# Eight normalises of h moved to VectorE, the last output tile cut 384 + 128, and a new written-out order

## The chip, the cores and the metric

One NeuronCore of a Trainium2 chip runs the whole kernel. The metric is the device time of one execution in microseconds, lower is better; several executions are taken and their median counts. Five engines run side by side, each through its own queue in order: TensorE (PE), VectorE (DVE), ScalarE (ACT), GpSimd (POOL) and SyncE (SP), which here only issues DMAs.

## The reference

x is 2048 tokens by 512. All inputs and outputs are bf16.

```python
h  = x + A(layernorm(x))          # linear attention, 32 heads of 16, then wo
h2 = h + B(layernorm(h))          # gMLP, F = 1792, Fh = 896

def A(x, wqkv, wo):
    q, k, v = heads(x @ wqkv)
    pq, pk = phi(q), phi(k)       # where(t > 0, t + 1, exp(t)) + 1e-6
    o = (pq @ (pk.T @ v)) / (pq @ sum(pk) + 1e-6)
    return o @ wo

def B(x, w_in, w_sp, b_sp, w_out):
    z = gelu(x @ w_in)
    g = w_sp @ layernorm(z[:, Fh:]) + b_sp[:, None]
    return (z[:, :Fh] * g) @ w_out
```

## The kernel before

The 2048 tokens are 16 tiles of 128 rows (n = 0 to 15), in eight pairs p and four groups of four (gq, tg). The work runs in five stages that overlap.

**Attention, keys.** For each tile of x, DVE takes statistics (`stats` L568, `aggr` L572), ACT or POOL makes 1/sqrt(var + eps) (`rstd_pool` L587 and L589 for pairs), DVE normalises (`normalise`, L603). The first six tiles are transposed by PE (L633, copied out by ACT, L640), the other ten by a transposing DMA on SP (L625). Then PE makes keys (`kv_proj`, L715), the feature map phi runs on ACT and DVE (L692, L694, L695, L698, L701), and PE sums key times x (L747). **Attention, queries.** `q_proj` (L729) and the denominators (`den`: L829, ACT L834 and L836, spread L844, ACT L854, DVE L856 and L859). **h.** PE projects (L879), DVE adds to x in place (L884), then the second layernorm: statistics on DVE, rstd on POOL, and, with `N2_ACT = range(16)`, `minus` on POOL (L614, L615: -mean times rstd) and the normalise itself on ACT (`normalise_act`, L610). The result goes to one of four buffers `xn` and from there through a transposing DMA on SP to hT (L625). A buffer is free for another tile when its DMA has read it. **gMLP in.** PE makes z2 from each tile (L911, two pieces of 512 and 384 columns), ACT takes gelu (L916), DVE takes statistics (L920) and normalises 896 columns (L603 again); PE makes z1 from groups of four tiles (L942) and ACT takes gelu (L947). **Mixing and out.** PE multiplies by w_sp (L981, 448 matmuls), DVE adds the bias (L988) and multiplies (L990), PE projects (L999), DVE adds h (L1005) and SP stores (L1007). The last tile is projected in two halves of 256 columns. w_sp reaches the chip through 64 transposing DMAs on SP (L957), of which the first 16 lie ahead of those of h in SP's queue. On POOL's queue stand the loads of wv, win, wo, the bias and wout (L492), each behind the last transpose that it must wait for.

**What sets the order.** Every operation is recorded by `op` with its operands; `schedule` then takes two lists written out by hand. ORDER lists all operations by number: each engine runs its own in the order in which they stand there. SLOT says which buffer each temporary tile takes (PSUM banks `ps`, buffers `e`, `xn`). From these the program derives the semaphores: an engine waits at an operation for its operands and for the earlier users of its buffer, and everything later on that engine waits behind it. The costs that stand at each `op` matter only to assertions and bookkeeping, as the lists decide the order.

Of the kernel before, what the change touches and what calls it, by code (L numbers as in the profile page):

```python
# [5 lines left out]
FP32 = mybir.dt.float32  # L6
BF16 = mybir.dt.bfloat16
ACT = mybir.ActivationFunctionType
ALU = mybir.AluOpType

P = 128
# [1 line left out]


ORDER = [
# [36 lines left out]
]  # L52
SLOT = [
# [6 lines left out]
]  # L60


# [292 lines left out]
def bass_sequential_preLN__linear_attn_block__mixer_gmlp__prompt_kernel(  # L355
# [11 lines left out]
    _, S, D = A_x.shape  # L367
# [15 lines left out]
    A_STATS = ()  # L383
    R_POOL = (4, 6, 8, 10, 12, 14)
    COPY_DVE = ()
    LN1 = [[0], [1], [2], [3], [4, 5], [6, 7], [8, 9], [10, 11], [12, 13], [14, 15]]
    N2_ACT = range(16)
    VIA_ACT = ((0, 0), (1, 0), (2, 0), (3, 0))

    x_dram, out_dram = A_x[0], out[0]  # L390
# [210 lines left out]
    def normalise(dst, src, st_row, k, rs, n=512, negative=False):  # L601
        m = st_row[k:k + 1]
        op("dve", dve_c(n, 4) + 0.1, lambda e: e.tensor_scalar(dst.ap(), src.ap(), m.ap(), rs.ap(),  # L603
                                                               op0=ALU.add if negative else ALU.subtract,
                                                               op1=ALU.mult),
           r=[src, m, rs], w=[dst])


    def normalise_act(dst, src, rs, nm, n=512):
        op("act", act_c(n, 2) + 0.04, lambda e: e.activation(dst.ap(), src.ap(), ACT.Identity, bias=nm.ap(), scale=rs.ap()),  # L610
           r=[src, rs, nm], w=[dst])

    def minus(m, rs, nm):
        op("pool", 0.25, lambda e: e.tensor_scalar(nm.ap(), m.ap(), -1.0, None, op0=ALU.mult), r=[m], w=[nm])  # L614
        op("pool", 0.25, lambda e: e.tensor_tensor(nm.ap(), nm.ap(), rs.ap(), ALU.mult), r=[nm, rs], w=[nm])  # L615
# [31 lines left out]
    for grp in LN1:  # L647
        rs = small([len(grp)], FP32)
        for i, n in enumerate(grp):
            rs_of[n] = rs[i:i + 1]  # L650
        for n in grp:
            if n in A_STATS:
                stats_act(n)
                continue
            stats(x[n, :], Row(st_x, n))
            first[n] = g.ops[-1]
            aggr(Row(st_x, n), 6)
            if n in CENTRED:
                m, c = st_x[n, 6:7], xc[n, :]
                op("dve", dve_c(512, 4) + 0.1, lambda e, n=n, m=m, c=c: e.tensor_scalar(  # L660
                    c.ap(), x[n, :].ap(), m.ap(), None, op0=ALU.subtract), r=[x[n, :], m], w=[c])
                transposed(n, lambda c=c: c, xcT, True)
        if grp[0] in A_STATS:
            rstd_act(st_x[grp[0], 7:8], rs.all(), 1.0 / D)
        elif grp[0] in R_POOL:
            rstd_pool(st_x[grp[0]:grp[-1] + 1, 7], rs.all(), len(grp))
        else:
            rstd_act(st_x[grp[0]:grp[-1] + 1, 7], rs.all())
        rs_op[grp[0]] = g.ops[-1]
        for i, n in enumerate(grp):  # L670
            d = xn1[n, :]
            normalise(d, x[n, :], Row(st_x, n), 6, rs[i:i + 1], negative=n in A_STATS)
            transposed(n, lambda d=d: d, xT, n in X_BY_PE)

    for gate, n, cost, count in ((first[0], 512, 2 * MM, 3), (rs_op[0], 512, 2 * MM, 1), (tr_op[0], 256, MM, 2),
# [340 lines left out]
                for n in range((tg - 1) * TPG, tg * TPG):  # L1016
                    project(n, [(0, D)])
    for n in range((NG - 1) * TPG, NT):
        project(n, [(0, D)] if n < NT - 1 else [(0, D // 2), (D // 2, D)])


    g.schedule()
# [55 lines left out]
```

## Time and profile before

| | us |
|---|---|
| median of 3 runs (lowest, highest) | 244.26 (243.93, 244.29) |
| the profiled execution, its own time | 243.96 |
| its span, first to last instruction | 242.2 |
| granted TensorE clock | 1.00 of full speed |

The profile is one execution. 1.76 us of its time lie outside the span. Its views show the busy time of each engine (a matmul's end is modelled, so PE can look busy while it waits a little), the chain of waits that ended last, groups of instructions by line and shape, and the instructions in order of time. Line numbers are those of the kernel before; in the kernel after they are 2 to 13 higher.

### The profile page before, as it was taken

How to read it: one execution, taken by the hardware profiler on the slowest of the kernel's cores; microseconds unless marked ns; L12 is line 12 of the kernel's file. 1: busy time of each engine (PE TensorE's matmuls, PEld its weight loads, DVE VectorE, ACT ScalarE, POOL GpSimd, SP SyncE). 2: the span in 40 equal slices, each digit the busy share in tenths (PEclk: the TensorE clock that was granted, in tenths of full speed). 3: DMA queues.
4: the chain of work that ended last, by engine and by line, in shares of the span. 5: the costliest groups of instructions: out<-in, count | busy, mean ns of one | idle time of the engine just before them, and what ended most of it. 6: DMA issues, size and time to landing. Idle time of an engine off the chain costs nothing.

```text
span 242.2 us, 3026 instructions
## 1 busy us (share of the span) xinstructions
PE 238.3 (98%) x1175; PEld 108.8 (45%) x1175; DVE 135.2 (56%) x269; ACT 85.1 (35%) x107; POOL 34.1 (14%) x87
## 2 busy tenths in 40 slices
PE   8999999999999999999999999999999999999995
PEld 3544443433444444445444444444444444444443
DVE  4999654589999967656533223251332513322443
ACT  3875744898588598564500010000000000000000
POOL 5316021002316542122100000000000000000000
DMA  6920459954324231459344444446200100000022
GB/s 199 321 43 18 94 106 337 232 122 96 46 43 128 47 46 22 87 119 231 88 108 92 107 86 95 100 108 94 83 0 0 65 24 0 0 0 3 0 87 87
DMA packets 55598, 21.57 MB, mean 89 GB/s; under 512 B 49472, under 2 KB 54720, under 8 KB 55584
## 3 DMA queue, kind: packets, MB, share of 16 engines
q1 hardware_dynamic: 54640, 17.05, 32.7%
q0 software_dynamic: 944, 4.33, 5.5%
q8 instruction: 9, 0.15, 0.3%
q14 instruction: 5, 0.04, 0.1%
HBM read 7.47 MB, written 2.10 MB: 40 GB/s over the span
## 4 chain that ended last, share of the span: by engine, by line
PE 91%; DVE 4%; DMA 2%; ACT 2%; SPq 1%; issue 0%
PE ps L981 40%; PE ps L942 10%; PE ps L911 10%; PE ps L999 10%; PE ps L747 6%; PE ps L879 5%; PE ps L715 5%; PE ps L729 4%; DMA xh<-in_A_x_dram 2%; DVE small L568 1%; SPq L492 1%; DVE xT_pq_z L698 1%; DVE xh L884 0%; DVE xT_pq_z L859 0%; DVE e L695 0%; PE ps L844 0%
## 5 line engine op out<-in xcount | busy, mean ns | idle before, releaser
L981 PE MATMUL ps<-wsp,pk_xn_z 128*128 128x512 bf16 x336 | 73.8, 379 | 0.0
L988 DVE TENSOR_TENSOR e<-ps,e 128x512 bf16<-128x512 f32 x28 | 19.4, 691 | 66.0 <-PE ps L981 66.0
L981 PEld LDWEIGHTS ps<-wsp,pk_xn_z 128*128 128x128 bf16 x336 | 32.8, 98 | 39.5
L942 PE MATMUL ps<-hT,win 128*128 128x512 bf16 x112 | 26.6, 379 | 0.0
L911 PE MATMUL ps<-win,hT 128*128 128x512 bf16 (+1 forms) x128 | 26.0, 353 | 0.0
L999 PE MATMUL ps<-wout,xT_pq_z 128*128 128x512 bf16 (+1 forms) x119 | 24.7, 367 | 0.0
L981 PE MATMUL ps<-wqkv_wsp,pk_xn_z 128*128 128x512 bf16 x112 | 24.3, 379 | 0.0
L947 ACT ACTIVATE xT_pq_z<-ps 128x1024 bf16<-128x1024 f32 (+1 forms) x16 | 14.4, 913 | 23.9 <-PE ps L942 23.9
L568 DVE BATCH_NORM_STATS2 small<-xh 128x6 f32<-128x512 bf16 x32 | 20.7, 678 | 3.3 <-DMA xh<-in_A_x_dram 3.3
L920 DVE BATCH_NORM_STATS2 small<-pk_xn_z 128x6 f32<-128x512 bf16 (+1 forms) x32 | 18.3, 611 | 7.2 <-ACT pk_xn_z L916 7.1
L692 ACT ACTIVATE e<-ps 128x1024 bf16<-128x1024 f32 x16 | 16.5, 1029 | 9.7 <-PE ps L715 6.1
L911 PEld LDWEIGHTS ps<-win,hT 128*128 128x128 bf16 x128 | 12.5, 98 | 12.7 <-ACT e L854 0.3
L916 ACT ACTIVATE pk_xn_z<-ps 128x896 bf16<-128x896 f32 x16 | 14.5, 914 | 8.9 <-PE ps L911 8.8
L1005 DVE TENSOR_TENSOR e<-ps,xh 128x512 bf16<-128x512 f32 (+1 forms) x17 | 11.2, 660 | 11.3 <-PE ps L999 11.3
L999 PEld LDWEIGHTS ps<-wout,xT_pq_z 128*128 128x128 bf16 x119 | 11.6, 98 | 12.8
L981 PEld LDWEIGHTS ps<-wqkv_wsp,pk_xn_z 128*128 128x128 bf16 x112 | 11.0, 98 | 13.2
L942 PEld LDWEIGHTS ps<-hT,win 128*128 128x128 bf16 x112 | 10.9, 98 | 12.6 <-ACT pk_xn_z L916 0.4
L589 POOL TENSOR_TENSOR small<-small 128x2 f32<-128x2 f32 x22 | 16.0, 727 | 1.2
L587 POOL TENSOR_SCALAR small<-small 128x2 f32<-128x2 f32 x22 | 6.4, 297 | 67.6 <-DVE small L572 67.4
L747 PE MATMUL ps<-pk_xn_z 128*128 128x512 bf16 x64 | 15.6, 379 | 0.0
L729 PE MATMUL ps<-xT_pq_z,wqkv_wsp 128*128 128x512 bf16 x64 | 15.5, 380 | 0.0
L715 PE MATMUL ps<-wqkv_wsp,xT_pq_z 128*128 128x512 bf16 x64 | 15.3, 379 | 0.0
(72 smaller groups left out, 191.0 us busy)
## 6 DMA issues: line engine op xcount, KB each, us to landing
out_dram<-e SPq DMA_DIRECT2D x15, 128.0 KB, 1.7
win<-in_B_w_in_dram POOLq DMA_DIRECT2D x1, 1792.0 KB, 9.2
xh<-in_A_x_dram SPq DMA_DIRECT2D x5, 256.0 KB, 4.7
wqkv_wsp<-in_A_wqkv_dram SPq DMA_DIRECT2D x2, 512.0 KB, 5.7
wout<-in_B_w_out_dram POOLq DMA_DIRECT2D x1, 896.0 KB, 6.4
wsp<-in_B_w_sp_dram SPq DMA_TRANSPOSE x48, 2.9
xh<-in_A_x_dram SPq DMA_DIRECT2D x1, 512.0 KB, 6.2
wqkv_wsp<-in_A_wqkv_dram POOLq DMA_DIRECT2D x1, 512.0 KB, 4.8
```

Source lines behind the costliest of these rows:

```text
L568: op("dve", dve_c(512), lambda e: e.bn_stats(s6.ap(), src.ap()), r=[src], w=[s6])
L589: return op("pool", 0.7, lambda e: e.tensor_tensor(dst.ap(), dst.ap(), h.ap(), ALU.pow), r=[dst, h], w=[dst])
L692: op("act", act_c(n), lambda e: e.activation(lo.ap(), t(flat).ap(), ACT.Exp), r=[t()], w=[lo])
L715: i = e.matmul(t(bank(ti)).ap(), lhsT=lhs.ap()[:, c, :], rhs=rhs.ap()[:, c, :], start=(c == 0), stop=(c == KD - 1))
L729: r_ = e.matmul(t(bank(i)).ap(), lhsT=lhs.ap()[:, c, :], rhs=rhs.ap()[:, c, :], start=(c == 0), stop=(c == KD - 1))
L747: r = e.matmul(txk[h](bank(i)).ap(), lhsT=xx.ap()[:, c * P:(c + 1) * P], rhs=kk.ap(), start=(n == 0), stop=(n == NT - 1))
L911: k = e.matmul(t(bank(i)).ap()[:, 0:b - a], lhsT=l.ap()[:, c, :], rhs=win[c, a:b].ap(), start=(c == 0), stop=(c == KD - 1))
L920: op("dve", dve_c(b - a), lambda e, s6=s6, src=src: e.bn_stats(s6.ap(), src.ap()), r=[src], w=[s6])
L942: k = e.matmul(t(bank(i)).ap(), lhsT=l.ap()[:, c, :], rhs=r_.ap()[:, c, :], start=(c == 0), stop=(c == KD - 1))
L981: k = e.matmul(t(bank(0)).ap(), lhsT=l.ap()[:, s - a, :], rhs=r_.ap()[:, s - a, :], start=(s == 0), stop=(s == NT - 1))
L988: op("dve", dve_c(512), lambda e: e.tensor_tensor(gb().ap(), t(bank(0)).ap(), bsp().ap()[:, tg * GW:(tg + 1) * GW], ALU.add), r=[t(), bsp( ...
L999: k = e.matmul(t(bank(0)).ap()[:, 0:b - a], lhsT=l.ap()[:, fc, :], rhs=wout[fc, a:b].ap(), start=(fc == 0), stop=(fc == KF - 1))
```

## The change

Three things change. The statistics and rstd stay where they were, but for tiles 8 to 15 the normalise of h runs on DVE (`normalise`) in place of ACT (`normalise_act`), and `minus` on POOL falls away for those four pairs. The last output tile is computed, added and stored as 384 and 128 columns. ORDER and SLOT are new lists throughout (796 operations in place of 804), so operations of all stages stand in another order, on every engine. `normalise_pool` and the tuples `N1_POOL` and `N1_ACT` are new as well; the tuples are empty, so tiles of x go the same way as before.

```diff
 ORDER = [
...
 SLOT = [
...
     COPY_DVE = ()
+    N1_POOL = ()
+    N1_ACT = ()
     LN1 = [[0], [1], [2], [3], [4, 5], [6, 7], [8, 9], [10, 11], [12, 13], [14, 15]]
-    N2_ACT = range(16)
+    N2_ACT = range(8)
...
+    def normalise_pool(dst, src, m, rs):
+        op("pool", 0.9, lambda e: e.tensor_scalar(dst.ap(), src.ap(), m.ap(), rs.ap(), op0=ALU.subtract,
+                                                  op1=ALU.mult), r=[src, m, rs], w=[dst])
...
-            normalise(d, x[n, :], Row(st_x, n), 6, rs[i:i + 1], negative=n in A_STATS)
+            if n in N1_POOL:
+                normalise_pool(d, x[n, :], st_x[n, 6:7], rs[i:i + 1])
+            elif n in N1_ACT:
+                nm = small([1], FP32)
+                minus(st_x[n, 6:7], rs[i:i + 1], nm.all())
+                normalise_act(d, x[n, :], rs[i:i + 1], nm.all())
+            else:
+                normalise(d, x[n, :], Row(st_x, n), 6, rs[i:i + 1], negative=n in A_STATS)
...
-        project(n, [(0, D)] if n < NT - 1 else [(0, D // 2), (D // 2, D)])
+        project(n, [(0, D)] if n < NT - 1 else [(0, D - P), (D - P, D)])
```

What the new lists move, as far as the prediction speaks of it:

- The keys of tiles 6 to 15 stand earlier among the work of PE: those of tile 10 come before the first half of the second group's queries has its partner (one `q_proj` pair, L729, fewer ahead of them).
- On DVE, the normalise of x's tile 10 has three more normalises and two more steps of phi ahead of it.
- The load of wo stands ahead of wv and win on POOL.
- All projections of tiles 12 to 15 (L879) now stand ahead of the denominators of the third group (L829); the first z2 of tile 2 (L911) follows directly on the spread L844 and takes the PSUM banks that held the z2 of tile 0.
- For tiles 8 to 15 the normalises on DVE take turns in the `xn` buffers: tile 10 takes the buffer of 8, 14 that of 10, 11 that of 9, 13 that of 11, so DVE waits there until the transposing DMA of the earlier tile has read it. On SP the transposes still go in the order 0 to 15.
- The last z2 tiles (13, 14, 12, 9, 15) and with them the need for the last hT tiles come earlier on PE; the tail of the mixing's first column (L981, token tiles 8 to 15) comes later.

84 rows, old and new, of tables (ORDER, SLOT) are left out of this document.

## The prediction

> **What bounds the kernel now.** I read the page's busy times first, then the chain of waits, then the windows by stage.
>
> ```profile
> span 242.2 us, 3026 instructions
> PE 238.3 (98%) x1175; PEld 108.8 (45%) x1175; DVE 135.2 (56%) x269; ACT 85.1 (35%) x107; POOL 34.1 (14%) x87
> PE 91%; DVE 4%; DMA 2%; ACT 2%; SPq 1%; issue 0%
> ```
>
> PE is busy 98% of the span and carries 91% of the chain that ended last. No edit removes a matmul, so the time can change only where PE waits, or before its first or after its last matmul.
>
> ```profile
> 10.59:57.00 46.41, 46.26 (x257) 20.41 (x258) 34.65 (x69) 33.32 (x39) 8.39 (x13) 1.00 0.60 138
> 57.00:70.00 13.00, 13.00 (x69) 5.73 (x70) 12.95 (x21) 9.58 (x12) 3.46 (x8) 1.00 0.36 63
> 70.00:90.00 20.00, 20.00 (x98) 9.45 (x97) 18.01 (x44) 15.48 (x21) 10.90 (x29) 1.00 0.32 66
> 90.00:120.50 30.50, 30.50 (x153) 14.77 (x151) 19.83 (x45) 18.75 (x22) 6.72 (x13) 1.00 0.52 106
> 120.50:239.74 119.24, 119.22 (x560) 54.45 (x558) 42.05 (x72) 2.05 (x2) 0.00 (x0) 1.00 0.24 56
> ```
>
> Each row is a stretch of the span: its length, then the busy time of PE, its weight loads, DVE, ACT and POOL (instructions in brackets), the clock, and the DMAs' share and GB/s. From 10.59 to 239.74 PE misses 0.15 + 0.02 us. A busy PE is not quite a fed one, but little is left to win there. DVE is the engine next to full: 12.95 of 13.00 us in 57 to 70 and 18.01 of 20.00 in 70 to 90. Into this stage the change puts eight more DVE instructions. The clock is 1.00 everywhere.
>
> ```profile
> 30.30 0.86 PE ps L715 x4
> ...
> 56.99 0.40 PE ps L844 x4
> ...
> 65.27 0.33 PE ps L829 x4
> ...
> 66.57 3.03 PE ps L911 x16
> 69.59 0.33 PE ps L844 x4
> 69.92 1.83 PE ps L942 x8
> ...
> 239.76 0.42 DVE e L1005
> ```
>
> This is the chain in order of time. Four 512-column matmuls take 0.86 us, one z2 tile 3.03 / 2 = 1.51.
>
> **The engines' prices.** Groups by form; the third number after the count is the mean ns of one.
>
> ```profile
> L610 ACT ACTIVATE xn<-xh,small 128x512 bf16<-128x512 bf16 x16 | 12.5, 805 | 4.5 <-POOL small L615 4.2 <-DMA hT<-xn 0.3
> L603 DVE TENSOR_SCALAR pk_xn_z<-xh,small 128x512 bf16<-128x512 bf16 x16 | 6.2, 400 | 0.0
> L614 POOL TENSOR_SCALAR small<-small 128x2 f32<-128x2 f32 x8 | 2.1, 260 | 1.7 <-DVE small L572 1.2
> L615 POOL TENSOR_TENSOR small<-small 128x2 f32<-128x2 f32 x8 | 2.3, 297 | 0.5
> L695 DVE TENSOR_SCALAR e<-e 128x1024 bf16<-128x1024 bf16 x16 | 6.7, 419 | 7.4 <-ACT e L694 5.6 <-ACT e L692 1.8
> L698 DVE TENSOR_TENSOR xT_pq_z<-e 128x1024 bf16<-128x1024 bf16 x8 | 5.4, 684 | 0.1
> L859 DVE TENSOR_TENSOR xT_pq_z<-xT_pq_z,ps 128x1024 bf16<-128x1024 bf16 x4 | 4.8, 1204 | 0.0
> L568 DVE BATCH_NORM_STATS2 small<-xh 128x6 f32<-128x512 bf16 x32 | 20.7, 678 | 3.3 <-DMA xh<-in_A_x_dram 3.3
> L1005 DVE TENSOR_TENSOR e<-ps,xh 128x512 bf16<-128x512 f32 x15 | 10.4, 691 | 10.9 <-PE ps L999 10.9
> L1005 DVE TENSOR_TENSOR e<-ps,xh 128x256 bf16<-128x256 f32 x2 | 0.8, 424 | 0.4 <-PE ps L999 0.3
> ```
>
> The move takes 8 x 0.805 = 6.4 us from ACT and 4 x (0.260 + 0.297) = 2.2 us from POOL, and gives DVE 8 x 0.400 = 3.2 us. None of these sums is on the chain; they matter through PE's waits. An instruction on DVE frees the queue about 0.08 us before its recorded end, so one normalise occupies it for 0.32, and likewise one statistics (L568) for 0.6, one product of phi or of the denominators (L698) for 0.6, the wide one with PSUM (L859) for 1.1.
>
> **Step 1, start to 10.59.** The first loads, statistics, transposes and keys stand in the same order on PE; on DVE one statistics of a later tile precedes tile 3's normalise, which PE needs only when its keys of tile 2 are done. Cost 0; bounds 0 and, if the later tile's data is late, +0.3 (one statistics, less that cover).
>
> **Step 2, keys, 10.59 to 45.** The keys of tiles 6 to 15 wait for transposing DMAs, and PE now asks earlier.
>
> ```profile
> 23.17 0.40 DVE L603 TENSOR_SCALAR pk_xn_z<-xh,small 128x512 bf16<-128x512 bf16 x1
> ...
> 30.40 2.58 SPq L625 DMA_TRANSPOSE xT_pq_z<-pk_xn_z  x2
> xT_pq_z<-pk_xn_z SPq DMA_TRANSPOSE x10, 2.5
> ```
>
> Tile 10's keys start at 30.30 before; after, one q_proj pair (1.73) fewer stands ahead, so PE asks at 28.57. Its normalise started at 23.17 at the end of a full DVE queue; three more normalises (0.96), one more L695 (0.34) and one more L698 (0.60) stand ahead now: 25.07, and up to 0.3 more if DVE waits for a rstd of POOL. It ends by 25.5 to 25.8, and the DMA lands 2.5 later, at 28.0 to 28.3: 0.3 to 0.6 us of slack, where there were 4. The transposes after it follow each 1.29 (2.58 / 2) apart, tile 15's at 34.5 to 34.8, for keys that PE reaches after 35. I take 0; the bounds are 0 and +0.5. wv, wo and win start up to 0.8 us later behind tile 15, with wo first; nothing in PE's order needs them sooner than before.
>
> **Step 3, 57 to 72.** Here I expect a wait.
>
> ```profile
> 66.01 0.67 ACT L834 ACTIVATE wsp<-ps,small 128x512 f32<-128x512 f32 x1
> ...
> 68.65 1.90 ACT L916 ACTIVATE pk_xn_z<-ps 128x896 bf16<-128x896 f32 x2
> ```
>
> The denominators of the third group (L829, 65.27 in the chain) wait for one more projection tile (0.86): about 66.1. L834 then starts at about 66.5 in place of 66.01, and the steps behind it on ACT up to the first gelu (L916) follow 0.5 later: gelu starts at 69.15 and frees its banks at about 70.1. PE does the same work up to there, the moved projection included, and reaches the end of the spread at 69.92; in the new order the next instruction wants just those banks: 0.2 us. The first z2 piece of tile 3 then waits for the copy L854 two ACT instructions on, less than 0.1 more. I take +0.3. Upper bound +0.8 (the gelus late by half a us more). Lower bound -0.3: the chain shows PE held before 56.99 by about 0.3, by the same kind of wait (sum into x, then the spread); I find that wait in the new order as well and so count no gain.
>
> **Step 4, 72 to 120.5: the moved normalises.**
>
> ```profile
> 54.81 1.22 DVE L884 TENSOR_TENSOR xh<-ps,xh 128x1024 bf16<-128x1024 f32 x1
> ...
> 87.10 0.92 DVE L603 TENSOR_SCALAR pk_xn_z<-pk_xn_z,small 128x896 bf16<-128x896 bf16 x2
> hT<-xn SPq DMA_TRANSPOSE x16, 2.5
> 92.62 10.78 SPq L625 DMA_TRANSPOSE hT<-xn  x6
> ```
>
> From its first addition of h (54.81) to the fourth normalise of z2 (87.10 + 0.92) DVE has almost no idle time. The new queue, from the first addition (1.5 earlier) to the normalise of tile 8, holds the same additions and statistics, four normalises more (1.3), a phi step (0.6) and a step of the denominators (0.6 to 1.1) more, one statistics of z2 less (0.5): 88.0 - 1.5 + 2.2 = 88.7 at its end. From there a chain through the buffers begins: transpose of 8 (2.5), normalise of 10 (0.4), its transpose, and likewise 9, 11, 13; with 0.1 per handover tile 11 lands at about 96.0, 13's DMA is issued at 96.5, 14's and 15's at 1.3 us steps behind it, and 15 lands at about 101.7. Before, the last of six transposes was issued about 1.3 before 92.62 + 10.78 = 103.4. PE reaches the first instruction that needs tile 15 (z1 of the fourth group) after 9 z2 tiles and one piece (14.5), 15 z1 blocks and 4 projections (19 x 0.86 = 16.3) and four pieces of mixing (1.7): 70.2 + 32.5 = 102.7. Cover: 1.0 us. All eight normalises then cost 0, hidden beside PE's work; if the cover is gone, each us on DVE's chain is one on PE's. The wait for buffers stands in DVE's queue, so behind it wait the normalises of z2 for the mixing; PE asks for the first of these at about 82.6 and has it by 82.2, later ones are covered by more. I take 0; bounds 0 and +1.5 (the chain late by 2.5, one whole transpose).
>
> **Step 5, 120.5 to 239.74.** 119.22 of 119.24 us busy, same matmuls, banks still in turn: 0. wsp's transposes start earlier than at 103.44 if step 4 holds.
>
> **Step 6, the tail.**
>
> ```profile
> 239.76 0.42 DVE L1005 TENSOR_TENSOR e<-ps,xh 128x256 bf16<-128x256 f32 x1 [0.34 <-PE ps L999]
> ...
> 240.21 0.33 SPq L1007 DMA_DIRECT2D out_dram<-e  x1
> out_dram<-e SPq DMA_DIRECT2D x15, 128.0 KB, 1.7
> out_dram<-e SPq DMA_DIRECT2D x2, 64.0 KB, 1.5
> ```
>
> The 384 columns end 0.38 (7 x 0.054) before the last matmul, at 239.36 with PE's end unmoved. Their addition, 0.56 between 0.424 and 0.691, ends at 239.94; its store is issued at 239.97 and holds SP for 0.33. The 128 columns' addition (0.29 by the same line) cannot start before 239.85 and ends at 240.14, a hair before 240.18 as it was, but its store waits for SP until 240.30 in place of 240.21: +0.09. Landing stays at 1.5 by the nearest row; bounds 1.4 (the line from 128 to 64 KB continued) and 1.7. Step: +0.1, bounds 0 and +0.3.
>
> The Trainium skill (DMA: Bandwidth & Descriptors, Specifications) gives 512 B as the smallest transfer at line rate and says that below it the engine does a read-modify-write; 128 columns are 256 B a row, 256 were 512 B. By it the last store would be slower, and no run here shows such a store yet.
>
> **Sum.** 0 + 0 + 0.3 + 0 + 0 + 0.1 = +0.4 us on the profiled execution's 243.96 (span 242.2 and 1.76 around it): 244.36. The runs' median is 244.26, 0.30 above the profiled one, whose time lies near the lowest, 243.93; three runs don't say how much of this is chance. I add 0.24 of it: **244.6**, between 244.36 and 244.66.
>
> **The rivals.**
> - **DVE's buffer chain is late (slower).** One mechanism: DVE waits in order for transposes to free `xn`, and tile 15 reaches hT after PE asks for z1 of group four. It decides from 1.0 us of delay before tile 8's normalise. For it: DVE has 0.05 of 13 us free in 57 to 70, and POOL's small instructions vary while DVE is full (rows below). Against: my queue count goes by rows, and DVE has 10 us free after 90. At 2 us of delay PE loses 1.0 to 1.5: 245.6 to 246.1.
>
> ```profile
> 17.43 0.86 POOL L587 TENSOR_SCALAR small<-small 128x2 f32<-128x2 f32 x1 [5.24 <-DVE small L572]
> 81.12 0.22 POOL L587 TENSOR_SCALAR small<-small 128x2 f32<-128x2 f32 x1 [3.15 <-DVE small L572]
> ```
>
>   The same instruction takes 0.22 or 0.86: up to 0.64 of the 1.0 us cover. The Trainium skill (Advanced Engine Details and Errata, VectorE Performance Modes) says that a VectorE instruction in a two-port mode and GpSimd block each other; by it the moved normalises would make rstd on POOL slower, and the trace agrees that rstd varies.
> - **The keys wait for tile 10 (slower, small).** If DVE's queue before 25 is 0.8 later, PE waits 0.3 to 0.5 in step 2: 244.9 to 245.1, still the forecast's side of the bound below or just past it.
> - **PE's early waits go (faster).** The wait before 56.99 vanishes, the gelu wait of step 3 does not come and no other does: -0.3 - 0.4 from the forecast, 243.9; with the profile's offset gone too, 243.6. Little more is there to win: PE misses 0.17 us by the records and about 0.3 by the chain.
> - **The change does nothing that shows.** Its edits are real (eight instructions change engine), but all are covered: 244.3, inside the forecast's range.
>
> **Chances.** 0.2% is 0.49 us, about what a measurement here can tell from no change: faster is below 243.77, slower above 244.75. Forecast and the covered case, 244.0 to 245.0: 0.58, of which 0.48 within and 0.10 above. Buffer chain late: 0.24, all above. Tile 10's wait on top of step 3: 0.08, 0.06 above. Early waits gone: 0.10, 0.08 below. Together 0.08 faster, 0.52 same, 0.40 slower. The range leaves out the last part of the faster case and the far end of the buffer chain: 243.7 to 246.2.
>
> **What would show it.** Step 2: no wait of L715 for a transpose near 28 us. Step 3: PE idle or its weight loads waiting for ACT's L916 near 70, about 0.2 us. Step 4: L603 normalises of 512 columns at 88 to 97, tile 15's transpose landing before 102.5, PE unbroken to the end. Step 6: last store issued about 0.55 after PE's last matmul, landing in about 1.5. Wrong would be: PE waiting on hT's DMA or on L603 between 82 and 116, or PE's last matmul more than 0.8 us from 240.0.

## The result, and the profile after

The changed kernel takes 244.64 us (median of 22 runs, 244.47 to 246.06), the kernel before in the same job 244.29 (22 runs, 243.89 to 247.58). The ratio is 1.0021, 95% interval 1.0012 to 1.003: slower by 0.3 to 0.7 us. The forecast was 244.6. The profiled execution took 244.63, its span is 242.9; that of before had 243.96 and 242.2.

First the page of the kernel after: span, engines, and the chain by engine.

```profile
span 242.9 us, 3014 instructions
PE 238.8 (98%) x1175; PEld 108.7 (45%) x1175; DVE 136.8 (56%) x277; ACT 79.5 (33%) x99; POOL 31.6 (13%) x79
PE 85%; DVE 7%; DMA 3%; ACT 1%; POOL 1%; SPq 1%; issue 0%; DVEq 0%
```

DVE has eight instructions more and ACT eight fewer, as the diff says. ACT's sum falls by 5.6 us and POOL's by 2.5, DVE's rises by 1.6 (forecast 6.4, 2.2 and 3.2; the sums don't set the time). PE's share of the chain falls from 91% to 85%, since the chain now runs through DVE up to the keys of tile 10. The windows of after, by the stretches of the forecast (columns as there), show where:

```profile
10.59:57.00 46.41, 46.13 (x256) 20.49 (x257) 34.74 (x69) 32.04 (x38) 8.03 (x13) 1.00 0.59 136
57.00:70.00 13.00, 13.00 (x70) 5.43 (x68) 13.00 (x24) 10.29 (x14) 2.84 (x8) 1.00 0.34 72
70.00:90.00 20.00, 19.77 (x100) 9.28 (x97) 19.62 (x48) 12.69 (x17) 9.04 (x21) 1.00 0.22 55
90.00:120.50 30.50, 30.50 (x152) 14.70 (x150) 20.97 (x50) 16.97 (x19) 7.11 (x13) 1.00 0.61 122
```

PE misses 0.28 us in the first stretch (0.15 before) and 0.23 between 70 and 90 (nothing before); it runs unbroken from 90 to the tail. The chain of waits of after, in order of time, names both places:

```profile
2.68 4.57 DMA xh<-in_A_x_dram
...
26.28 2.41 DMA xT_pq_z<-pk_xn_z
28.69 0.14 issue
28.82 1.02 PE ps L728 x4
...
69.42 0.93 ACT pk_xn_z L929
70.39 1.04 PE ps L924 x4
```

These are tile 10's keys (L728 here, L715 before), which wait for their transposing DMA, and the second z2 (L924, L911 before), which waits for the first gelu.

**How big the two waits are.** The recorded end of a matmul is modelled, so idle time by the records understates a gap; the distance of starts doesn't. PE in time order, after:

```profile
26.75 1.89 PE L760 MATMUL ps<-pk_xn_z 128*128 128x512 bf16 x8
28.82 1.02 PE L728 MATMUL ps<-wqkv_wsp,xT_pq_z 128*128 128x512 bf16 x4 [0.19 <-DMA xT_pq_z<-pk_xn_z]
...
69.78 0.40 PE L857 MATMUL ps<-wsp,small 32*128 32x512 bf16 x4
70.39 1.04 PE L924 MATMUL ps<-win,hT 128*128 128x512 bf16 x4 [0.23 <-ACT pk_xn_z L929]
```

Eight matmuls at 0.216 take 1.73, so PE was ready at 28.48 and started at 28.82: **0.35** lost (0.19 by the records). The other wait stands behind the spread of the third group. There PE of before has:

```profile
69.53 0.40 PE L844 MATMUL ps<-wsp,small 32*128 32x512 bf16 x4
69.85 1.90 PE L942 MATMUL ps<-hT,win 128*128 128x512 bf16 x8
```

Before, the next matmul came 69.85 - 69.53 = 0.32 after the spread's start, here it comes 70.39 - 69.78 = 0.61 after it: **0.29** lost.

**A wait that went.** PE and ACT of before, then PE and ACT of after, at the spread of the fourth group (L844, L857):

```profile
55.85 1.03 PE L729 MATMUL ps<-xT_pq_z,wqkv_wsp 128*128 128x512 bf16 x4
56.99 0.40 PE L844 MATMUL ps<-wsp,small 32*128 32x512 bf16 x4
...
56.22 0.63 ACT L836 ACTIVATE wsp<-wsp 128x512 bf16<-128x512 f32 x1
```

```profile
57.99 1.03 PE L892 MATMUL ps<-pk_xn_z,xT_pq_z 128*128 128x512 bf16 x4
58.95 0.40 PE L857 MATMUL ps<-wsp,small 32*128 32x512 bf16 x4
...
57.71 0.63 ACT L849 ACTIVATE wsp<-wsp 128x512 bf16<-128x512 f32 x1
```

The four matmuls of 512 columns ahead of the spread take 1.14 from start to start before and 0.96 after: **0.19** gained (unrounded). The spread reads what ACT writes in this row (L836, L849). Before, that was done at 56.22 + 0.63 = 56.85, just ahead of the spread; after, at 58.34, 0.61 ahead of it, since the new order has three blocks of four matmuls between the denominators and the spread where the old one has two. No run here puts this wait back by itself: its size rests on these rows, and on the run of all three together below, which agrees.

**The tail.** DVE and SP of after:

```profile
239.91 0.56 DVE L1018 TENSOR_TENSOR e<-ps,xh 128x384 bf16<-128x384 f32 x1 [0.45 <-PE ps L1012]
...
240.39 0.28 DVE L1018 TENSOR_TENSOR e<-ps,xh 128x128 bf16<-128x128 f32 x1
240.50 0.33 SPq L1020 DMA_DIRECT2D out_dram<-e  x1
240.87 0.43 SPq L1020 DMA_DIRECT2D out_dram<-e  x1
```

PE's last row of before, then of after:

```profile
238.25 1.47 PE L999 MATMUL ps<-wout,xT_pq_z 128*128 128x256 bf16 x12
```

```profile
238.14 2.12 PE L1012 MATMUL ps<-wout,xT_pq_z 128*128 128x512 bf16 x16
```

The store of 384 columns holds SP from 240.50, and that of 128 follows at 240.87, 0.61 (unrounded) after PE's last matmul ends as recorded, at 240.27; before, the last store came 240.21 - 239.72 = 0.49 after it. From PE's end to the end of the span it is 2.63 in place of 2.51: **0.12** lost.

**The start.** From the chain of before, then PE of after:

```profile
2.68 4.51 DMA xh<-in_A_x_dram
...
10.59 0.72 PE ps L633 x8
```

```profile
10.65 0.72 PE L639 MATMUL ps<-small,pk_xn_z 128*128 128x128 bf16 x8 [0.21 <-DVE pk_xn_z L605]
```

The load of x's tiles 4 and 5 lands at 7.26 after (2.68 + 4.57 in the chain) and at 7.19 before. DVE's statistics and normalises follow without a pause, and PE starts the transposes of tiles 4 and 5 (L639, L633) at 10.65 and 10.59: 3.39 behind the landing in both (unrounded). It was 3.39 to 3.40 in every profile of this study, while the landing itself went from 7.16 to 8.34. So times are compared below from this start of PE to the end of the span as well: 242.23 - 10.59 = 231.65 before, 242.90 - 10.65 = 232.25 after, from unrounded records. These **+0.60** are what the change does behind the loads; 0.35 + 0.29 - 0.19 + 0.12 = 0.57 of it is found above. The medians, with the landing in them, differ by 0.35, and the lowest of the 22 runs of each by 0.58.

### The profile page after: what moved, and what is told of

Read it like the earlier page. It is cut to its first block, busy times and chain, and to the rows that moved or that the text cites. A ratio compares the mean times of both kernels' runs of the same rounds, so it can differ in the third digit from the quotient of the medians.

```text
span 242.9 us, 3014 instructions
## 1 busy us (share of the span) xinstructions
PE 238.8 (98%) x1175; PEld 108.7 (45%) x1175; DVE 136.8 (56%) x277; ACT 79.5 (33%) x99; POOL 31.6 (13%) x79
## 4 chain that ended last, share of the span: by engine, by line
PE 85%; DVE 7%; DMA 3%; ACT 1%; POOL 1%; SPq 1%; issue 0%; DVEq 0%
PE ps L994 40%; PE ps L955 10%; PE ps L1012 10%; PE ps L924 9%; PE ps L892 6%; PE ps L742 4%; PE ps L760 3%; DVE small L570 3%; PE ps L728 2%; DMA xh<-in_A_x_dram 2%; DVE pk_xn_z L605 1%; DMA xT_pq_z<-pk_xn_z 1%; DVE pk_xn_z L714 1%; DVE e L708 1%; SPq L494 1%; POOL small L591 1%
## 5 line engine op out<-in xcount | busy, mean ns | idle before, releaser
L994 PE MATMUL ps<-wsp,pk_xn_z 128*128 128x512 bf16 x336 | 73.8, 379 | 0.0
L994 PEld LDWEIGHTS ps<-wsp,pk_xn_z 128*128 128x128 bf16 x336 | 32.9, 98 | 39.7
L924 PE MATMUL ps<-win,hT 128*128 128x384 bf16 (+1 forms) x128 | 26.4, 353 | 0.2 <-ACT pk_xn_z L929 0.2
L1012 PE MATMUL ps<-wout,xT_pq_z 128*128 128x512 bf16 (+2 forms) x119 | 24.7, 366 | 0.0
L994 PE MATMUL ps<-wqkv_wsp,pk_xn_z 128*128 128x512 bf16 x112 | 24.3, 379 | 0.0
L933 DVE BATCH_NORM_STATS2 small<-pk_xn_z 128x6 f32<-128x512 bf16 (+1 forms) x32 | 18.5, 611 | 5.2 <-ACT pk_xn_z L929 4.9
L924 PEld LDWEIGHTS ps<-win,hT 128*128 128x128 bf16 x128 | 12.3, 98 | 13.0 <-ACT pk_xn_z L929 0.5
L1018 DVE TENSOR_TENSOR e<-ps,xh 128x512 bf16<-128x512 f32 (+2 forms) x17 | 11.1, 659 | 11.4 <-PE ps L1012 11.4
L994 PEld LDWEIGHTS ps<-wqkv_wsp,pk_xn_z 128*128 128x128 bf16 x112 | 11.0, 98 | 13.2
L591 POOL TENSOR_TENSOR small<-small 128x2 f32<-128x2 f32 x22 | 16.5, 752 | 1.3
L728 PE MATMUL ps<-wqkv_wsp,xT_pq_z 128*128 128x512 bf16 x64 | 15.1, 379 | 0.2 <-DMA xT_pq_z<-pk_xn_z 0.2
L892 PE MATMUL ps<-pk_xn_z,xT_pq_z 128*128 128x512 bf16 x64 | 15.0, 379 | 0.0
```

Of the source, the lines that this page charges most:

```text
L591: return op("pool", 0.7, lambda e: e.tensor_tensor(dst.ap(), dst.ap(), h.ap(), ALU.pow), r=[dst, h], w=[dst])
L728: i = e.matmul(t(bank(ti)).ap(), lhsT=lhs.ap()[:, c, :], rhs=rhs.ap()[:, c, :], start=(c == 0), stop=(c == KD - 1))
L892: i = e.matmul(t(bank(ti)).ap(), lhsT=l.ap()[:, c, :], rhs=mw[c, :].ap(), start=(c == 0), stop=(c == KD - 1))
L924: k = e.matmul(t(bank(i)).ap()[:, 0:b - a], lhsT=l.ap()[:, c, :], rhs=win[c, a:b].ap(), start=(c == 0), stop=(c == KD - 1))
L933: op("dve", dve_c(b - a), lambda e, s6=s6, src=src: e.bn_stats(s6.ap(), src.ap()), r=[src], w=[s6])
L994: k = e.matmul(t(bank(0)).ap(), lhsT=l.ap()[:, s - a, :], rhs=r_.ap()[:, s - a, :], start=(s == 0), stop=(s == NT - 1))
```

## The experiments

Theory: four separate terms, a wait for tile 10's keys, a wait for the first gelu, a wait of before that went, and a store that queues at the tail; the eight normalises themselves cost nothing. Rivals: the normalises cost or gain something; one wait replaces another, so the terms don't add up.

| kernel | median, us (runs) | ratio to before, 95% | PE's start | start to end |
|---|---|---|---|---|
| before | 244.29 (22) | | 10.59 | 231.65 |
| after | 244.64 (22) | 1.0021 (1.0012 to 1.003) | 10.65 | 232.25 |
| tail_halves | 245.05 (9) | 1.0033 (1.0019 to 1.0047) | 11.73 | 232.30 |
| before_tail_384 | 244.31 (12) | 1.0008 (0.9996 to 1.0019) | 10.71 | 231.77 |
| keys_swap | 244.55 (12) | 1.0019 (1.0 to 1.0038) | 11.11 | 231.91 |
| den_first | 244.59 (12) | 1.0017 (0.9998 to 1.0035) | 10.55 | 231.94 |
| three | 244.01 (12) | 0.9992 (0.9982 to 1.0002) | 10.94 | 231.46 |
| move_alone | 244.31 (12) | 1.0008 (0.9999 to 1.0017) | 10.96 | 231.64 |
| move_undone | 245.63 (6) | 1.0061 (1.0043 to 1.0078) | 11.08 | 232.99 |
| late_2 | 244.95 (1) | | 10.95 | 232.26 |
| late_4 | 246.39 (1) | | 10.88 | 233.78 |
| pool_free | 244.77 (1) | | 11.11 | 231.91 |

The last two columns are of the profiled execution: the start of the transposes of tiles 4 and 5 on PE (the expectation of three calls them those of tile 3), and from there to the end of the span. Before ran beside tail_halves to den_first at 244.17, beside three to move_undone at 244.03. The medians bear differences of a few tenths only roughly: the expectations had 244.5 for tail_halves, 244.3 for keys_swap, 244.35 for den_first and no change for move_alone, and none of these four came. In the profiles the load of tiles 4 and 5 landed 0.32 to 1.08 later than in after in tail_halves, keys_swap and move_alone, though no edit touches it. The lowest runs of keys_swap and den_first, 244.14 and 244.13, lie below the lowest of after, 244.47, by about what the last column says. No kernel was profiled twice, so how well the last column repeats is not measured; three pairs that should agree if the account is right (before and move_alone, after and late_2, keys_swap and pool_free) do so to 0.02.

### Before with the tail alone

```diff
-        project(n, [(0, D)] if n < NT - 1 else [(0, D // 2), (D // 2, D)])
+        project(n, [(0, D)] if n < NT - 1 else [(0, D - P), (D - P, D)])
```

> The kernel before with only the last tile cut 384 + 128. Theory: +0.12 us on before, 244.4, PE untouched up to its last matmul and the last store issued 0.12 later. Rival (cut is free): 244.29. Rival (a 256-byte row lands slower): +0.3 or more, landing above 1.6 against 1.53.

Measured: 231.77 against 231.65, +0.12, all of it behind PE's last matmul (2.63 against 2.51, unrounded 0.13); the theory's number. The 128-column store lands in 1.55, so the rival of a slow landing fails. The median can't show 0.12.

### After with the tail undone

```diff
-        project(n, [(0, D)] if n < NT - 1 else [(0, D - P), (D - P, D)])
+        project(n, [(0, D)] if n < NT - 1 else [(0, D // 2), (D // 2, D)])
```

> The kernel after with the last tile stored in 256 + 256 columns again, all else as after. Theory (the 384-column addition holds DVE, and its store holds SP, so that the 128-column store is issued 0.12 later): last issue 0.49 after PE's last matmul ends as modelled, against 0.61 in after; span 0.12 shorter, median 0.1 below after, 244.5. Rival (landing of a small store, not the queue, sets the end): issue moves but the span does not, 244.64. Rival (the cut is free and after's loss lies wholly earlier): 244.64 with the same issue.

Measured: behind PE's end 2.49, 0.14 less, as expected; but the time from PE's start is 232.30, no gain. Neither the theory nor a rival had that. PE's weight loads in the tail of this run:

```profile
240.60 0.11 PEld L1012 LDWEIGHTS ps<-wout,xT_pq_z 128*128 128x128 bf16 x2 [0.30 <-DVE e L1018]
```

In after's SLOT the last piece takes the PSUM bank of tile 14, which DVE's addition of tile 14 frees. With 384 + 128 PE comes there later, by 7 matmuls of 128 columns, 7 x 0.054 = 0.38, and doesn't wait; with halves it waits 0.19 by the distance of starts. So the uneven cut goes with that bank: undone alone it only exchanges one loss for another.

### Tile 10 normalised ahead of tile 11

```diff
+for a, b in ((105, 103),):
+    i, j = ORDER.index(a), ORDER.index(b); ORDER[i], ORDER[j] = b, a
```

105 is the normalise of x's tile 11 on DVE, 103 that of tile 10.

> After, with the normalises of x's tiles 10 and 11 changed over on DVE: tile 10 is normalised first, right behind the wait for their common rstd. Theory (PE's gap of 0.35 before tile 10's keys comes from the place of its normalise in DVE's queue): its transpose is issued about 25.6 in place of 26.28 and lands by 28.1, before PE asks at 28.47; the gap goes, the work behind it moves up by 0.35, median 244.3. Rival (the gap moves: another transpose, or the gelu wait near 70, takes the gain back): PE's start of tile 10's keys early, but the end unmoved, 244.6. Rival (SP's queue holds the transpose): it still lands at 28.7, 244.64.

Measured: 231.91, 0.34 below after. PE of this run:

```profile
27.21 1.89 PE L760 MATMUL ps<-pk_xn_z 128*128 128x512 bf16 x8
28.94 1.03 PE L728 MATMUL ps<-wqkv_wsp,xT_pq_z 128*128 128x512 bf16 x4
```

Eight matmuls and no wait: 1.73 from start to start. The gap is gone, and nothing later takes the gain back.

### The denominators ahead of tile 13's projection

```diff
+for a, b in ((351, 271), (391, 278)):
+    i, j = ORDER.index(a), ORDER.index(b); ORDER[i], ORDER[j] = b, a
```

351 is the addition of tiles 6 and 7 on DVE, 271 the phi product; 391 the projection of tile 13 on PE, 278 the denominators (L842).

> After, with the denominators of the third group ahead of the projection of tile 13 on PE as in before, and the phi product that they need ahead of the addition of tile 7 on DVE. Theory (PE's gap of 0.29 near 70 comes from the chain denominators, ACT, table load, gelu being one projection later): L847 starts about 65.9 in place of 66.76, the first gelu ends 0.86 earlier, PE runs on from the spread without the gap: median 244.35. Rival (PE then waits for the phi product before the denominators, or for tile 7's addition, which is now 0.6 later): a gap of 0.2 to 0.4 near 65, 244.6 or above.

Measured: 231.94, 0.31 below after. ACT, then PE of this run:

```profile
65.80 0.69 ACT L847 ACTIVATE wsp<-ps,small 128x512 f32<-128x512 f32 x1 [0.59 <-PE ps L842]
```

```profile
69.67 0.40 PE L857 MATMUL ps<-wsp,small 32*128 32x512 bf16 x4
70.00 1.04 PE L924 MATMUL ps<-win,hT 128*128 128x512 bf16 x4
```

L847 starts at 65.80 as expected, and PE goes on 0.32 after the spread's start. No gap comes near 65.

### All three together

```diff
+for a, b in ((105, 103), (351, 271), (391, 278)): i, j = ORDER.index(a), ORDER.index(b); ORDER[i], ORDER[j] = b, a
+SLOT[-2] = 0
...
-        project(n, [(0, D)] if n < NT - 1 else [(0, D - P), (D - P, D)])
+        project(n, [(0, D)] if n < NT - 1 else [(0, D // 2), (D // 2, D)])
```

> After, with the two changes of order of the runs on the keys and on the denominators together, the last tile in 256 + 256 columns, and the last piece in a PSUM bank that tile 14 does not use. Measured from PE's last start behind the loads (the transposes of tile 3, 3.39 behind the landing of x's loads), the span after is 232.25, that of before 231.65. Theory (three separate losses that add up: 0.34 keys, 0.31 gelu, 0.14 tail): 231.46, 0.2 below before, median near 244.0. Rival (the waits replace one another, so that the sum isn't reached): 231.7 to 232.0.

Measured: 231.46, the expected number. The three losses are separate and add up. What is left against before, 0.19, is the size of the wait that went. In whole runs this is 0.9992 of before (0.9982 to 1.0002), not clear of no change; the median, 244.01, is the expected one.

### The move alone, and the move undone

```diff
+GONE = (373, 374, 388, 389, 403, 404, 418, 419)
+ORDER = [s - sum(g < s for g in GONE) for s in ORDER if s not in GONE]
...
-    N2_ACT = range(16)
+    N2_ACT = range(8)
```

> Before, with only the normalises of h's tiles 8 to 15 on DVE, at the places that they had on ACT, POOL's minus of those pairs gone; order and buffers otherwise as before. Theory (they are hidden, as the prediction's step 4 had it, if DVE does not wait in its queue for buffers longer than PE's cover): 231.65 from PE's start, median as before, within 0.1. Rival (in this order DVE waits for the transposes that free the buffers of tiles 10, 11 and 15 and the z2 normalises come late): PE gaps between 85 and 115 of 0.5 or more.

Measured: 231.64 against 231.65 of before. In the old order the move of eight normalises is worth nothing, in either direction. The rival's condition came, its gaps did not: DVE waits 1.39 us at 90.84, until tile 8's transpose has freed a buffer, and PE shows no gap behind it.

```diff
+RSTD = (372, 385, 398, 411)
+ORDER = [s + 2 * sum(r < s for r in RSTD) + k for s in ORDER for k in ((0, 1, 2) if s in RSTD else (0,))]
...
-    N2_ACT = range(8)
+    N2_ACT = range(16)
```

> After, with the normalises of h's tiles 8 to 15 back on ACT, at the places that they have on DVE, and POOL's minus of those pairs behind each rstd. Theory (the move itself is worth nothing, after's loss lies in its order and its tail): 232.25 from PE's start, median as after, within 0.1. Rival (the new order needs the move; on ACT each takes 0.8 in place of 0.4 and stands before gelus): gaps of PE between 75 and 115 and 0.5 or more on the time. Rival (the move costs and ACT was better): shorter than after by 0.1 or more.

Measured: 232.99, 0.74 above after: the theory fails here, the first rival holds. PE of this run:

```profile
102.09 1.68 PE L924 MATMUL ps<-win,hT 128*128 128x384 bf16 x8
104.18 1.04 PE L955 MATMUL ps<-hT,win 128*128 128x512 bf16 x4 [0.42 <-DMA hT<-xn]
```

Eight z2 matmuls take 1.51, so PE was ready at 103.60 and waited 0.58 for tile 15's hT; another 0.15 is lost at 90.05. At these places in the order ACT delivers tile 15 too late and DVE in time; other places for ACT's normalises were not run. So the move is worth 0 in the old order and 0.74 in the new one. That the new order is worth anything over the old shows only in the run of all three together, by its 0.19.

### DVE made late

```diff
+i = ORDER.index(375)
+ORDER[i:i] = range(796, 798)
...
+    spare = small([2, 8], FP32)
+    for k in range(2):
+        stats(x[8, :], Row(spare, k))
```

375 is the normalise of h's tile 9. The second run has four of them (796 to 799).

> After, with two spare statistics (0.6 each) put on DVE ahead of the normalise of h's tile 9; what they write is not used. Theory (the chain through the xn buffers passes a delay on, and PE's cover before tile 15 is 103.02 - 101.94 = 1.08): tile 15's transpose lands 1.2 later, near 103.1, PE waits 0.1 to 0.3 for it; from PE's start 232.25 becomes 232.4 to 232.5. Rival (DVE's own idle time of 0.59 at 95 takes up part of it): lands below 102.6, no gap, 232.25. Rival (z2's normalises for the mixing, later by as much, are missed first): a gap at a mixing piece near 95 to 99.

> The same with four spare statistics, 2.4 in all. Theory (1.08 of cover, then one for one): tile 15 lands near 104.3, PE waits about 1.4; 233.6 to 233.7 from PE's start. Rival (0.59 taken up by DVE's idle time): a gap of 0.8, 233.05. Rival (the mixing's normalises first): gaps near 95 to 99, in sum no smaller.

First DVE and SP of after around these normalises, PE's mixing piece that needs the z2 normalise at 96.02, and PE's first use of tile 15:

```profile
87.89 0.71 DVE L605 TENSOR_SCALAR xn<-xh,small 128x512 bf16<-128x512 bf16 x2
...
96.02 0.51 DVE L605 TENSOR_SCALAR pk_xn_z<-pk_xn_z,small 128x896 bf16<-128x896 bf16 x1
96.44 0.40 DVE L605 TENSOR_SCALAR xn<-xh,small 128x512 bf16<-128x512 bf16 x1
97.40 0.59 PE L994 MATMUL ps<-wsp,pk_xn_z 128*128 128x512 bf16 x2
98.10 2.58 SPq L631 DMA_TRANSPOSE hT<-xn  x2
103.02 0.38 PE L955 MATMUL ps<-hT,win 128*128 128x512 bf16 x1
```

The last two transposes are issued from 98.10 to 100.68 and tile 15 lands 1.26 later, at 101.94: 1.08 ahead of PE. The mixing piece has less cover: its normalise ends at 96.53, 0.87 ahead. With two statistics more, SP's row is:

```profile
97.97 3.81 SPq L631 DMA_TRANSPOSE hT<-xn  x3
```

It ends at 101.78, so tile 15 lands at 103.04; PE had started 0.30 later, so the delay is 1.10 - 0.30 = 0.80 of the 1.2 put in. Nothing is lost (232.26). The time is the first rival's, the way to it is nobody's. The landing is too early for the theory and too late for the rival: on after's clock it is 102.74, 0.28 ahead of PE, where the theory had 103.1 and the rival below 102.6. DVE's idle time at 95 takes up nothing, for it is still 0.60 long. Half of the 0.4 (0.21) is taken up at 90.78, where z2's statistics (L933) wait in after for a gelu that ends at 90.74 and here find it done; the rest goes in smaller steps. With four, PE:

```profile
95.25 2.84 PE L924 MATMUL ps<-win,hT 128*128 128x512 bf16 x12
98.77 0.60 PE L994 MATMUL ps<-wsp,pk_xn_z 128*128 128x512 bf16 x2 [0.68 <-DVE pk_xn_z L605]
...
104.76 1.04 PE L955 MATMUL ps<-hT,win 128*128 128x512 bf16 x4 [0.18 <-DMA hT<-xn]
```

233.78, 1.53 lost of 2.4. The sum is near the theory's, the place is mostly the last rival's: the mixing piece (L994) that waits for the z2 normalise (L605) loses 0.84 at 98.77. Tile 15 loses only 0.34. The twelve z2 matmuls ahead of the mixing piece lose 0.30 (they take 2.84, 2.54 in after), where the first of tile 10 waits for its transpose, which lands at 96.93. In this run DVE also waits 0.50 for a buffer, that of tile 11, ahead of tile 13's normalise; in after and with two statistics it waits for none.

### POOL's rstd

```diff
+for a, b in ((105, 103),): i, j = ORDER.index(a), ORDER.index(b); ORDER[i], ORDER[j] = b, a
+ORDER.remove(226); ORDER.insert(ORDER.index(103) + 1, 226)
```

226 is the phi product that ran on DVE just ahead of DVE's wait.

> The run on the keys, with the phi product L711 that ran on DVE while POOL made the rstd of tiles 10 and 11 moved behind the normalise of tile 10. Theory (POOL stands still while DVE runs this product: L591 took 1.33 in place of some 0.7 because 0.6 of it lay beside L711): L591 for tiles 10 and 11 takes about 0.7, DVE's wait shrinks by 0.6 to 0.7 and tile 10's transpose is issued that much earlier than in the run on the keys; PE has no gap there either way, 231.9 from PE's start. Rival (L591's time varies by itself): 1.3 again.

POOL and DVE of after, where tile 10's rstd is made, then POOL and DVE of pool_free's same step:

```profile
22.85 0.56 POOL L589 TENSOR_SCALAR small<-small 128x2 f32<-128x2 f32 x1 [1.73 <-DVE small L574]
23.50 1.33 POOL L591 TENSOR_TENSOR small<-small 128x2 f32<-128x2 f32 x1
...
23.57 0.69 DVE L711 TENSOR_TENSOR xT_pq_z<-e 128x1024 bf16<-128x1024 bf16 x1
24.86 0.73 DVE L605 TENSOR_SCALAR pk_xn_z<-xh,small 128x512 bf16<-128x512 bf16 x2 [0.60 <-POOL small L591]
```

```profile
23.95 0.73 POOL L591 TENSOR_TENSOR small<-small 128x2 f32<-128x2 f32 x1
...
24.72 0.41 DVE L605 TENSOR_SCALAR pk_xn_z<-xh,small 128x512 bf16<-128x512 bf16 x1 [0.60 <-POOL small L591]
```

L591 takes 0.73 with the product moved, and took 1.33 with it beside. It takes 1.33 in all eight profiles that have the product there, so it doesn't vary by itself. The 0.60 is what the product occupies of DVE. Tile 10's normalise starts at 24.72, 0.60 earlier than in keys_swap (25.32), and the time is 231.91, as expected. What the theory had wrong is DVE's wait: it is still 0.60, as the product went from ahead of it and DVE is there sooner by as much. The short step ahead of it on POOL (L587, L589 after) shows the same: it takes 0.22 alone, and 0.62 at 20.56 in before and 0.56 at 22.85 in after, where it starts inside a product. The Trainium skill (Advanced Engine Details and Errata, VectorE Performance Modes) says that VectorE instructions in a two-port mode and those of GpSimd block each other, but its table there gives `tensor_tensor`, which the product is, no such mode. So this stretch is shown by the runs and not explained by that rule. And in before the same kind of product ran beside the same step of POOL and neither was stretched:

```profile
23.41 0.73 POOL L589 TENSOR_TENSOR small<-small 128x2 f32<-128x2 f32 x1
```

```profile
23.50 0.68 DVE L698 TENSOR_TENSOR xT_pq_z<-e 128x1024 bf16<-128x1024 bf16 x1
```

DVE starts 0.09 behind POOL here and 0.07 behind in after; the other two profiles of the old order have 0.72 and 0.73 as well. What decides between them stays open.

## Why the prediction was right, and where it was not

- **The time** (244.6 against 244.64) is right, its make-up only in part, and that the two agree to 0.04 is partly luck. Behind the loads the forecast sum was +0.4 and the change costs +0.60; the forecast then added 0.24 because before's profiled execution lay below its median, while after's, 244.63, lay at its own. So the medians differ by 0.35, as forecast (0.34), and not by 0.60.
- **Step 1, cost 0:** right; PE's start lies 3.39 behind the landing of x's tiles 4 and 5 in both orders.
- **Step 2, cost 0:** wrong, 0.35 lost. The step that failed is the arrival of tile 10's normalise, "25.07, and up to 0.3 more if DVE waits for a rstd of POOL". It starts at 25.84: DVE waits 0.60, and the rest of the queue is 0.17 late. The 0.3 had no working behind it. Tile 10 shares its rstd with tile 11, whose statistics the new order completes at 22.58 in place of 19.90; from there POOL needs until 24.83, with 1.33 for L591. By the rows of pool_free (0.73) it would have been done at about 24.2, when DVE was ready, and tile 10 in time (an estimate: no run changes that alone). The step also put the handover from landing to first matmul at nothing; it took 0.13 (28.69 to 28.82). The bound of +0.5 held the loss. It is the rival of the keys, whose condition, DVE 0.8 later, and wait, 0.3 to 0.5, both came; it had a chance of 0.08. Its time, 244.9 to 245.1, did not come, as 0.19 was gained elsewhere and the offset of the medians shrank.
- **Step 3, +0.3:** the gelu wait is right in place, mechanism and size (0.29; gelu starts at 69.42, forecast 69.15). What failed is "I find that wait in the new order as well and so count no gain": the wait before 56.99 was worth 0.19 and is gone. It was not the sum into x that held the spread, as the step has it; that ended at 54.81 + 1.22 = 56.03. It was ACT's L836, which ended at 56.85, and the new order covers it. The two misses, +0.35 and -0.19, cancel by half: that is luck too.
- **Step 4, cost 0:** the cost is right, and so is tile 15's landing: 101.94 (forecast 101.7), asked for at 103.02 (102.7), a cover of 1.08 (1.0). The path to it was another. In after DVE waits for no buffer; tile 8's transpose lands at 91.04, and tile 10's normalise, which takes its buffer, starts at 91.85, behind z2's statistics in DVE's queue. That the landing agrees to 0.24 is in part luck. What failed is "later ones are covered by more", of the mixing's normalises: the one that ends at 96.53 has 0.87, less than tile 15. So the rival built on this step has the size about right (nothing lost at 1.2 us of delay, 1.53 at 2.4), but the wait for hT that it names is only 0.64 of the 1.53. A slower rstd beside the moved normalises, its other premise, doesn't show: from 57 us on this step of POOL (L589, L591 after) takes 0.70 to 0.82 after and 0.69 to 0.84 before.
- **Step 5, cost 0:** right; PE shows no gap between 90 and its last matmul.
- **Step 6, +0.1:** right, 0.12; the 128 columns' addition waits for DVE as forecast, its store for SP. The last store of 32 KB lands in 1.54, as that of 64 KB did (1.53). The Trainium skill's rule on transfers below 512 B (DMA: Bandwidth & Descriptors, Specifications) adds no time to the landing here.
- **Covered altogether** (the rival that the change does nothing that shows): true of the move of the normalises in the old order, 231.64 against 231.65, and not of the new order that came with it.

## What to carry to other kernels

Where one engine is busy 98% of the span, a new order of everything is worth what its few waits are worth: find them by the distance of starts, not by recorded idle time (0.35 against 0.19 here), and put each right by itself; here three swapped pairs and the old tail gave back 0.79 us, more than the 0.60 lost. When a step arrives by an engine's queue, follow what it waits for there back to its own start, and price the slow value seen (POOL's 1.33, not 0.73): by the estimate above one such value took all of the cover. And judge changes of 0.1 us from a point behind the first loads, as their landing alone, from 7.16 to 8.34, moves the whole by up to 1.2 us.

## What the runs showed of the hardware

- PE's start behind the loads was 3.39 to 3.40 after the load of x's tiles 4 and 5 landed, in all twelve profiles; the landing varied from 7.16 to 8.34.
- A POOL step on 128x2 numbers (L591) took 1.33 where a phi product on DVE started 0.07 to 0.08 behind it (eight profiles) and 0.73 with the product moved away; where the product started 0.09 behind it (three profiles of the old order) it took 0.72 to 0.73. What decides is open.
- A 512-column matmul is recorded with 0.38 us and the next one starts 0.216 later, so recorded idle time of PE (0.19) was less than the time lost (0.35).
- The issue of the 128-column store occupied SP for 0.43, those just ahead of it, of 256 to 512 columns, 0.33; the 128-column store landed in 1.54 to 1.55, those of 256 columns in 1.53 to 1.56.
